# Linear attention: the product with the key-value state folded into the output weight, inverse denominators broadcast through DRAM; Mixer 1 held in program order

## The chip, the cores and the metric

The kernel runs on one core of one Trainium2 chip. The metric is the device time of one execution in microseconds (us). A kernel is timed in several rounds beside the kernel before on the same chip.

Engine names as the profile prints them: PE is TensorE (matmuls), PEld its weight loads, DVE is VectorE, ACT is ScalarE, POOL is GpSimd, SP is SyncE, which here only issues DMAs. L1163 is line 1163 of the kernel concerned; line numbers differ a little between the kernels.

## The reference, cut to what matters

A pre-normalised block: linear attention over 2048 tokens (width 1024, 32 heads of 32), then a token-mixing MLP with 3584 hidden features.

```python
phi = lambda t: jnp.where(t > 0, t + 1, jnp.exp(t)) + 1e-6
pq, pk = phi(q), phi(k)
kv  = jnp.einsum("bhsd,bhse->bhde", pk, v)          # one 32x32 state per head
z   = jnp.einsum("bhsd->bhd", pk)
num = jnp.einsum("bhqd,bhde->bhqe", pq, kv)
den = jnp.einsum("bhqd,bhd->bhq", pq, z)[..., None] + 1e-6
o   = num / den
h   = x + o.reshape(B, S, D) @ wo                   # q, k, v are projections of layernorm(x)
# Mixer: y = w2(gelu(w1(layernorm(h), over tokens) + b1)) + b2;   result = h + y
```

Because the division is by one number for each token and head, it may be done on `pq`, before both products. Then `kv` and `wo` can be multiplied together once, and the output projection takes the scaled `pq` directly.

## The kernel before

The work runs in this order on TensorE: keys and values with their state; the query projection in 32 units of eight matmuls (a unit is 512 tokens by 128 features); the attention product and the output projection in 16 row blocks of 128 tokens; Mixer 1 (2048 tokens to 3584 features, a seven-product matrix scheme nested in quads, five quads after the first pair); Mixer 2.

The attention product works on one row block: eight matmuls of 132 columns (numerator and denominator side by side), two small ScalarE operations for 1/den as exp(-ln), three VectorE products, and a transposing DMA back into `pqT`.

```python
def attn_num_den(i):
    for j in range(ND):                                   # 8 matmuls, 132 columns each
        nc.tensor.matmul(nd_ps[:, b, sl * NCOL:(sl + 1) * NCOL],
                         lhsT=pqT[:, j, i * P:(i + 1) * P], rhs=ndrhs[:, j, :], start=True, stop=True)
    nc.scalar.activation(dn..., nd_ps..., ACT.Ln, bias=eps_den[:], scale=1.0)
    nc.scalar.activation(rd[:], dn[:], ACT.Exp, scale=-1.0)
    ...                                                   # 3 VectorE products into o_sb
def attn_transpose(i, o_sb):
    nc.sync.dma_start_transpose(out=pqT[:, :, i * P:(i + 1) * P], in_=o_sb[:])

def out_proj(i):
    ...
    for dc in range(NDC):                                 # two halves of 512 columns
        ap_ = acc_tile()                                  # one of five PSUM tiles, in a ring
        nc.scalar.copy(ap_[:, 0:CW], xr[:, dc * CW:(dc + 1) * CW])     # seed: x into PSUM
        for j in range(ND):
            nc.tensor.matmul(ap_[:, 0:CW], lhsT=pqT[:, j, i * P:(i + 1) * P],
                             rhs=wo_sb[:, j, dc * CW:(dc + 1) * CW], ...)
        nc.scalar.copy(h_bf[:, dc * CW:(dc + 1) * CW], ap_[:, 0:CW])
        nc.vector.bn_stats(st[:, dc, :], ap_[:, 0:CW])
    nc.vector.bn_aggr(mv_all[:, i, :], st[:])
    nc.scalar.activation(lnv[:], mv_all[:, i, 1:2], ACT.Ln, ...)       # then Exp
    nc.sync.dma_start(h_dram[i][:], h_bf[:])

for (u, j) in q_units[8:]:
    q_unit(u, j)                                          # 8 matmuls, then phi on ScalarE and VectorE
    if u >= 1 and j % 2 == 1:
        i = (u - 1) * TPC + j // 2
        attn(i)
        ...                                               # loads of wo, then of w1
for i in range(NS):
    if i % 2 == 0 and i // 2 < TPC:
        attn(NS - TPC + i // 2)
    load_xr(i + XRL)                                      # cut: only while there are rows left
    out_proj(i)
    if i >= 2: normalize_h(i - 2)                         # layer norm, then combinations of row pairs
    ...
```

A scheduler sets each engine's order from this program. `pin(...)` holds an instruction in program order against the other pinned ones of its engine; what is not pinned may move.

## Time and profile before

572.96 us median of 3 runs (572.88 to 573.27). The profiled execution has a span of 571.5 us.

From the page: busy time by engine, then the busy share of TensorE and its granted clock in 40 equal slices, in tenths.

```profile
PE 563.7 (99%) x3124; PEld 293.3 (51%) x3124; DVE 390.2 (68%) x759; ACT 272.0 (48%) x585; POOL 1.8 (0%) x8
PE   7999999999999999999999999999999999999997
PEclk9999999999999999999999999999999999999999
```

TensorE is the limit: nothing pays that doesn't take time off it. The next view is the table of windows. I cut the span at four events in TensorE's trace: the last key-value matmul, the first matmul of Mixer 1, the first quad, the end of the quads and the first matmul of Mixer 2. Columns: window, length, then busy time (and instructions) of each engine, granted clock, DMA share, GB/s.

```profile
125.86:235.50 109.64, 109.64 (x604) 53.47 (x602) 85.99 (x208) 74.87 (x178) 0.00 (x0) 1.00 0.61 158
235.50:259.32 23.82, 22.93 (x106) 10.18 (x106) 18.33 (x35) 10.35 (x18) 0.00 (x0) 1.00 0.03 12
259.32:376.01 116.69, 116.52 (x673) 65.60 (x672) 62.90 (x129) 56.00 (x119) 0.00 (x0) 1.00 0.29 91
376.01:403.03 27.02, 27.02 (x153) 14.86 (x152) 10.37 (x19) 13.00 (x27) 0.00 (x0) 1.00 0.27 69
```

The first window is the attention stage (queries, attention product, output projection): 109.64 us, and TensorE is busy in all of it. The second is the start of Mixer 1, with 0.9 us of waiting. The third holds five quads, 22.42 us and then four of 23.57 us. "The stage", "the mixer start" and "the quads" mean these windows below.

TensorE's timeline around two attention groups (start, length, instruction, count):

```profile
150.23 0.63 PE L1118 MATMUL nd_ps<-ndrhs,pqT 128*128 128x132 bf16 x8
150.70 3.61 PE L1019 MATMUL acc_t<-xnT,wq_sb 128*128 128x512 bf16 x16
154.15 0.63 PE L1118 MATMUL nd_ps<-ndrhs,pqT 128*128 128x132 bf16 x8
```

A group of eight attention matmuls takes 0.47 us of TensorE's time (150.23 to 150.70); there are 16 groups, 7.5 us.

### The profile page before, as it was taken

To read this page: it belongs to the slowest core of one execution; us is meant where nothing else is said; L and a number is where in the kernel's file an instruction comes from. 1 tells how busy PE (TensorE), PEld (TensorE's weight loads), DVE (VectorE), ACT (ScalarE), POOL (GpSimd) and SP (SyncE) were. 2 spreads that over 40 slices of the span, in tenths; PEclk is the share of its full clock that TensorE was granted. 3 is DMA by queue.
4 is the path that set the end of the run, shared out by engine and by line. 5 is a ranking of instruction groups with operands and counts; after the bars stand their busy time and mean duration, and the time that the engine had idled before them with its cause. 6 is when DMAs were issued, how large, how long until landed. Compare 5 with 4: busy or idle time off the path is not lost.

```text
span 571.5 us, 8308 instructions
## 1 busy us (share of the span) xinstructions
PE 563.7 (99%) x3124; PEld 293.3 (51%) x3124; DVE 390.2 (68%) x759; ACT 272.0 (48%) x585; POOL 1.8 (0%) x8
## 2 busy tenths in 40 slices
PE   7999999999999999999999999999999999999997
PEld 3444444455554444346555565555445655645643
DVE  6898887546767879873735627453979749659625
ACT  4747777666667776445445354453220411311211
POOL 1000000000000000000000000000000000000000
PEclk9999999999999999999999999999999999999999
DMA  9933432029536753104041340413892932912111
GB/s 303 357 76 79 89 74 38 19 96 323 118 72 127 177 178 111 55 2 147 1 148 28 120 148 1 148 48 81 205 255 84 244 96 75 278 56 73 38 47 46
DMA packets 97800, 66.61 MB, mean 117 GB/s; under 512 B 32082, under 2 KB 91744, under 8 KB 97760
## 3 DMA queue, kind: packets, MB, share of 16 engines
q1 hardware_dynamic: 97024, 65.42, 41.7%
q10 hardware_dynamic: 672, 0.66, 0.3%
q8 instruction: 24, 0.39, 0.3%
q14 instruction: 16, 0.13, 0.1%
q0 software_dynamic: 64, 0.01, 0.0%
HBM read 50.34 MB, written 8.39 MB: 103 GB/s over the span
## 4 chain that ended last, share of the span: by engine, by line
PE 95%; DVE 3%; ACT 1%; issue 1%; DMA 1%; ACTq 0%
PE psB L297 10%; PE psC L297 10%; PE acc_t L1019 9%; PE acc_t L1167 9%; PE psC L208 7%; PE psA L297 7%; PE psI L230 7%; PE psB L208 6%; PE psI L208 6%; PE psB L750 4%; PE psC L750 4%; PE psA L750 4%; PE psA L208 3%; PE acc_t L674 2%; PE psE L750 2%; PE psE L297 1%
## 5 line engine op out<-in xcount | busy, mean ns | idle before, releaser
L297 PEld LDWEIGHTS <-sa 128*128 128x128 f16 x436 | 42.6, 98 | 46.8 <-issue 0.7
L1019 PE MATMUL acc_t<-xnT,wq_sb 128*128 128x512 bf16 x256 | 58.0, 379 | 0.0
L1167 PE MATMUL acc_t<-wo_sb,pqT 128*128 128x512 bf16 x256 | 56.1, 379 | 0.0
L208 PEld LDWEIGHTS <-wq 128*128 128x128 bf16 (+1 forms) x357 | 34.5, 98 | 31.3
L297 PEld LDWEIGHTS <-wq 128*128 128x128 bf16 (+1 forms) x324 | 31.6, 98 | 33.1 <-issue 1.0
L208 PE MATMUL psC<-gs,wq 128*128 128x512 f16 (+2 forms) x210 | 45.0, 365 | 0.0
L1167 PEld LDWEIGHTS <-pqT 128*128 128x128 bf16 x256 | 24.8, 98 | 29.0
L1019 PEld LDWEIGHTS <-wq_sb 128*128 128x128 bf16 x256 | 24.5, 98 | 27.4
L166 ACT ACTIVATE e_sb<-acc_t 128x512 bf16<-128x512 f32 x40 | 23.9, 597 | 26.5 <-PE acc_t L1019 24.3
L170 DVE TENSOR_SCALAR e_sb<-e_sb 128x512 bf16<-128x512 bf16 x64 | 18.5, 289 | 25.4 <-ACT e_sb L166 24.8
L208 PEld LDWEIGHTS <-sa 128*128 128x128 f16 x231 | 22.6, 98 | 18.6
L750 PEld LDWEIGHTS <-xs 128*128 128x128 f16 x208 | 20.0, 98 | 23.3 <-DVE xs L736 1.3
L208 DVE TENSOR_TENSOR ot<-ot,hr 128x512 bf16<-128x512 bf16 (+2 forms) x27 | 11.2, 415 | 28.1 <-ACT ot L406 27.7
L333 ACT COPY psC<-psB 128x512 f32<-128x512 f32 x22 | 12.5, 570 | 35.1 <-PE psB L297 21.5
L297 PE MATMUL psB<-hT,sa 128*128 128x512 f16 x112 | 28.4, 379 | 0.0
L441 DVE TENSOR_TENSOR e<-psI,es 128x256 f32<-128x256 f32 x12 | 5.1, 425 | 34.0 <-PE psI L230 34.0
L297 PE MATMUL psC<-hT,wq 128*128 128x512 f16 x112 | 28.3, 379 | 0.0
L750 PE MATMUL psA<-wkv,xnT 128*128 128x512 bf16 x104 | 26.7, 379 | 0.0
L1178 DVE BATCH_NORM_STATS2 hst<-acc_t 128x6 f32<-128x512 f32 x32 | 22.1, 692 | 6.7 <-ACT h_bf L1177 6.5
L297 PE MATMUL psA<-hO,wq 128*128 128x512 f16 x112 | 25.6, 379 | 0.7 <-ACT psB L316 0.7
L297 PE MATMUL psB<-hO,sa 128*128 128x512 f16 x112 | 25.5, 379 | 0.0
L297 PE MATMUL psC<-hT,sa 128*128 128x512 f16 x112 | 25.5, 379 | 0.0
(184 smaller groups left out, 1022.9 us busy)
## 6 DMA issues: line engine op xcount, KB each, us to landing
wq<-in_B_w_dram SPq DMA_DIRECT2D x14, 1024.0 KB, 7.7
wq<-in_B_w_dram SPq DMA_DIRECT2D x8, 1792.0 KB, 9.1
xr<-in_A_x_dram SPq DMA_DIRECT2D x16, 256.0 KB, 3.1
h_dram<-h_bf SPq DMA_DIRECT2D x16, 256.0 KB, 2.2
hr<-h_dram SPq DMA_DIRECT2D x32, 128.0 KB, 2.4
out_dram<-ot SPq DMA_DIRECT2D x31, 128.0 KB, 1.8
x_sb<-in_A_x_dram SPq DMA_DIRECT2D x15, 256.0 KB, 3.2
wkv<-in_A_wqkv_dram SPq DMA_DIRECT2D x2, 1024.0 KB, 9.0
```

Source lines behind the costliest of these rows:

```text
L166: pin(nc.scalar.activation(e_sb[:], src, ACT.Exp))
L170: pin(nc.vector.tensor_scalar(e_sb[:], e_sb[:], 1.0, PHI_EPS, ALU.min, ALU.add))
L208: return (lambda *a, **kw: pin(op(*a, **kw))) if Held.on else op
L230: pe.matmul(ps, lhsT=self.lhs[m][:, k, :], rhs=self.mov[m][:, k, :], start=(start and k == 0), stop=(k == self.nk - 1), skip_group_check=True,
L297: pe.matmul(ps[:, cols], lhsT=lhs[:, k, :], rhs=mv(k)[:, cols], start=(start and k == 0), stop=(k == self.nk - 1), skip_group_check=True,)
L333: nc.scalar.copy(self.C[:], self.B[:])
L441: dve.tensor_tensor(self.sts[m].e[:, self.cols(h)], ps, es, ALU.add)
L674: mm = nc.tensor.matmul(pp[:, 0:CW], lhsT=xnT[:, kt, i * P:(i + 1) * P], rhs=wkv[:, kt, c * CW:(c + 1) * CW], start=(kt == 0), stop=(kt == ...
L750: pin(nc.tensor.matmul(ps[:], lhsT=lhs[:, k, :], rhs=rhs[:, k, :], start=(start and k == 0), stop=(k == hk2 - 1), skip_group_check=True,))
L1019: nc.tensor.matmul(qp[:, 0:SW], lhsT=wq_sb[:, kt, j * P:(j + 1) * P], rhs=xnT[:, kt, u * SW:(u + 1) * SW], start=(kt == 0), stop=(kt == ND ...
L1167: nc.tensor.matmul(ap_[:, 0:CW], lhsT=pqT[:, j, i * P:(i + 1) * P], rhs=wo_sb[:, j, dc * CW:(dc + 1) * CW], start=(j == 0 and not SEED_RES ...
L1178: nc.vector.bn_stats(st[:, dc, :], ap_[:, 0:CW])
```

## The change

The intent is to take the 128 attention matmuls (and 48 VectorE products) away. The state is transposed and multiplied into the output weight once (`kv_transpose`, `fold`). The denominators of a chunk of 512 tokens come from eight matmuls of 32 output rows that can run four at a time in column groups of the array. Their inverses go to DRAM and come back broadcast over the 32 features of each head (`rdb`), and two VectorE products for each chunk scale `pqT` in place. Independently of this, the additions of Mixer 1's quads are held in program order. The diff, cut to its core:

```diff
-            def attn_num_den(i): ...          # 8 matmuls, Ln, Exp, 3 products
-            def attn_transpose(i, o_sb): ...
+            def kv_transpose():               # 8 transposes, one ScalarE copy
+                ...
+            def fold(j):
+                for c in range(NDC):
+                    ps = acc_tile()
+                    nc.tensor.matmul(ps[:, 0:CW], lhsT=kvT[:, j, :], rhs=wo_sb[:, j, cols], start=True, stop=True)
+                    ...                       # copied into wf by ScalarE (c == 0) or VectorE
+            def den(u):
+                ps = ndp.tile([P, SW], F32, tag="den", name="den_ps")
+                for o in range(2):
+                    for g in range(4):
+                        j = 4 * o + g
+                        nc.tensor.matmul(
+                            ps[g * QR:(g + 1) * QR, :],
+                            lhsT=zz[:, j, (1 - o) * HB:(1 - o) * HB + QR],
+                            rhs=pqT[:, j, u * SW:(u + 1) * SW], ...
+                            tile_position=(0, g * QR),
+                        )
+                nc.scalar.activation(ps[:], ps[:], ACT.Ln, bias=eps_den[:], scale=1.0 / S)
+                nc.scalar.activation(rd[:], ps[:], ACT.Exp, scale=-1.0)
+                pin(nc.sync.dma_start(rd_dram[u][:], rd[:]))
+                for h in range(2):
+                    rdb = a3d.tile([P, NH, SW], FP16, tag="rdb", bufs=3, name="rdb")
+                    for q in range(HB):
+                        pin(nc.sync.dma_start(rdb[q * DH:(q + 1) * DH, :, :], ... to_broadcast([DH, 4, SW])))
+                    rdbs[u, h] = rdb
+                    if 0 < u < 3:
+                        load_w1(u - 1, h, pin)            # 1 MB each
+            def scale_q(u, h):
+                v = pqT[:, h * NH:(h + 1) * NH, u * SW:(u + 1) * SW]
+                pin(nc.vector.tensor_tensor(v, v, rdbs.pop((u, h))[:], ALU.mult))
...
+            scale_at = {6: (0, 0), 7: (0, 1), 13: (1, 0), 14: (1, 1), 21: (2, 0), 22: (2, 1)}
+            for n, (u, j) in enumerate(q_units[8:]):
                 q_unit(u, j)
-                if u >= 1 and j % 2 == 1: attn(i) ...
+                if j == 0:
+                    den(u - 1)
+                if n == 1:
+                    kv_transpose()
+                if 4 <= n < 4 + ND:
+                    fold(n - 4)
+                if n in scale_at:
+                    scale_q(*scale_at[n])
             for i in range(NS):
-                if i % 2 == 0 and i // 2 < TPC: attn(NS - TPC + i // 2)
+                if i == 0:
+                    den(NSC - 1)
+                elif i in (3, 4):
+                    scale_q(NSC - 1, i - 3)
...
# Mixer 1: additions of a quad through `dve`, which is pinned while Held.on
-            nc.vector.tensor_tensor(t[:], ps[:], self.e[:], ALU.add)
+            dve.tensor_tensor(t[:], ps[:], self.e[:], ALU.add)
...
+    nxt.hold = pin
+    Held.on = True
     for u in range(1, NQ1):
         ...
+    Held.on = False
```

More of the change, by code (lines that the diff above doesn't have):

```diff
@@ L56 @@
     HB = P // DH
-    NCOL = P + HB
-    JPB = BANK // NCOL
-    NNB = (ND + JPB - 1) // JPB
+    QR = P // 4
+    assert ND == 8 and 3 * HB <= QR
     KPB = BANK // (P + 1)
@@ L100 @@
     for q in range(HB):
-        nc.vector.memset(maskbd[q * DH:(q + 1) * DH, q * DH:(q + 1) * DH], 1.0)
+        nc.vector.memset(maskbd[q * DH:(q + 1) * DH, q * DH:(q + 1) * DH], 1.0 / S)
         nc.vector.memset(m4[q * DH:(q + 1) * DH, q:q + 1], 1.0)
@@ L107 @@
     eps_den = const.tile([P, 1], F32)
-    nc.vector.memset(eps_den[:], DEN_EPS)
+    nc.vector.memset(eps_den[:], DEN_EPS / S)
     b1_rows = const.tile([NF, P], BF16)
@@ L134, in w_tile, with load_w1 @@
         return pool.tile([P, n], BF16, tag="wq", name="wq")
-    def load_w1(u, half):
+    def load_w1(u, half, hold=lambda ins: ins):
         if half == 0:
@@ L139, in load_w1 @@
         k = slice(half * NSP, (half + 1) * NSP)
-        nc.sync.dma_start(
+        hold(nc.sync.dma_start(
             w1_tiles[u][:, k, :],
             B_w1[:, u * CW:(u + 1) * CW].rearrange("(k p) f -> p k f", p=P)[:, k, :],
-        )
+        ))
     def load_w2(p, pool):
@@ L218, in __init__, with sums @@
             self.lhs = {1: self.a11, 2: self.a12, 4: self.a22}
-        def sums(self):
+        def sums(self, hold=lambda ins: ins):
             sm = [pools["is"].tile([P, self.nk, P], FP16, tag=self.tag, bufs=pools["is_bufs"], name="is")[:] for _ in range(4)]
-            dve.tensor_tensor(sm[0], self.a21, self.a22, ALU.add)
+            hold(dve.tensor_tensor(sm[0], self.a21, self.a22, ALU.add))
             dve.tensor_tensor(sm[1], sm[0], self.a11, ALU.subtract)
@@ L373, in evac_shared, with finish @@
             t = pools["t"].tile([P, BANK], F32, tag=f"t{fh}", name="t1")
-            nc.vector.tensor_tensor(t[:], ps[:], self.e[:], ALU.add)
+            dve.tensor_tensor(t[:], ps[:], self.e[:], ALU.add)
             self.evac(fh, 1, t)
+        todo = []
         def done(self):
-            e = gE[:, self.p, :]
-            nc.vector.tensor_tensor(e[:, CW:D], e[:, CW:D], e[:, 0:CW], ALU.subtract)
+            self.todo.append(gE[:, self.p, :])
+            if not Held.on:
+                self.finish()
+        def finish(self):
+            while self.todo:
+                e = self.todo.pop(0)
+                dve.tensor_tensor(e[:, CW:D], e[:, CW:D], e[:, 0:CW], ALU.subtract)
     class Mixer2(Product7):
@@ L422, in __init__ @@
             self.mov1, self.mov5 = mov1, mov5
+            self.hold = lambda ins: ins
         def cols(self, h):
@@ L445, in pre @@
                 self.in1 = Inner(self.sts, 1, self.mov1, "i1", self.sink1, self.sum1)
-                self.in1.sums()
+                self.in1.sums(self.hold)
             for st in self.sts:
@@ L530, in run @@
             interleave(self.in5, [st.p6 for st in self.sts])
+            self.sts[0].finish()
             pre = nxt.pre if nxt is not None else (lambda m: None)
@@ L585 @@
         a3s = actx.enter_context(tc.tile_pool(name="a3s", bufs=4))
-        a3w = actx.enter_context(tc.tile_pool(name="a3w", bufs=3))
-        a3o = actx.enter_context(tc.tile_pool(name="a3o", bufs=3))
+        a3d = actx.enter_context(tc.tile_pool(name="a3d", bufs=1))
         hstat = actx.enter_context(tc.tile_pool(name="hstat", bufs=1))
@@ L594 @@
         pqT = pqpool.tile([P, ND, S], BF16)
-        ndrhs = pqpool.tile([P, ND, NCOL], BF16)
+        kvbd = pqpool.tile([P, ND, P], BF16)
+        zz = pqpool.tile([P, ND, QR + HB], BF16)
         xctx = ExitStack()
@@ L1084 @@
                 q_fill()
+            nc.vector.memset(zz[:, :, 0:3 * HB], 0.0)
+            nc.vector.memset(zz[:, :, 3 * HB:], float(S))
             for b in range(NKB):
@@ L1087 @@
                 nc.vector.tensor_tensor(
-                    ndrhs[:, j0:j0 + n, 0:P],
+                    kvbd[:, j0:j0 + n, :],
                     kv_ps[b][:, 0:n, 0:P],
@@ L1093 @@
                 nc.vector.tensor_tensor(
-                    ndrhs[:, j0:j0 + n, P:NCOL],
+                    zz[:, j0:j0 + n, HB:2 * HB],
                     kv_ps[b][:, 0:n, P:P + 1].to_broadcast([P, n, HB]),
@@ L1101 @@
         warmctx.close()
+        kvT = xctx.enter_context(tc.tile_pool(name="kvtpool", bufs=1)).tile([P, ND, P], FP16, name="kvT")
         wpool = sactx.enter_context(tc.tile_pool(name="wpool", bufs=2, side="right"))
@@ L1109 @@
         ndp = a3p.enter_context(tc.tile_pool(name="ndp", bufs=1, space=PSUM))
-        nd_ps = ndp.tile([P, NNB, BANK], F32, name="nd_ps")
-        nc.vector.memset(nd_ps[:], 0.0)
+        rd_dram = [dram.tile([P, SW], FP16, name=f"rd_dram{u}") for u in range(NSC)]
         with ExitStack() as a3:
-            def attn_num_den(i):
+            def kv_transpose():
+                tp = ndp.tile([P, ND, P], BF16, tag="tp", name="kvtp")
                 for j in range(ND):
-                    b, sl = divmod(j, JPB)
-                    nc.tensor.matmul(
-                        nd_ps[:, b, sl * NCOL:(sl + 1) * NCOL],
-                        lhsT=pqT[:, j, i * P:(i + 1) * P],
-                        rhs=ndrhs[:, j, :],
-                        start=True,
-                        stop=True,
-                    )
-                dn = a3s.tile([P, NNB * JPB * HB], F32, name="dn")
-                nc.scalar.activation(
-                    dn[:].rearrange("p (b s c) -> p b s c", b=NNB, c=HB),
-                    nd_ps[:, :, 0:JPB * NCOL].rearrange("p b (s c) -> p b s c", c=NCOL)[:, :, :, P:NCOL],
-                    ACT.Ln,
-                    bias=eps_den[:],
-                    scale=1.0,
-                )
-                rd = a3s.tile([P, NNB * JPB * HB], F32, name="rd")
-                nc.scalar.activation(rd[:], dn[:], ACT.Exp, scale=-1.0)
-                o_sb = a3o.tile([P, D], BF16, name="o_sb")
-                for b in range(NNB):
-                    nsl = min(JPB, ND - b * JPB)
-                    blk = nd_ps[:, b, 0:nsl * NCOL].rearrange("p (s c) -> p s c", c=NCOL)
-                    nc.vector.tensor_tensor(
-                        o_sb[:, b * JPB * P:(b * JPB + nsl) * P].rearrange("p (s h e) -> p s h e", h=HB, e=DH),
-                        blk[:, :, 0:P].rearrange("p s (h e) -> p s h e", e=DH),
-                        rd[:, b * JPB * HB:(b * JPB + nsl) * HB].rearrange("p (s h) -> p s h", h=HB).unsqueeze(3).to_broadcast([P, nsl, HB, DH]),
-                        ALU.mult,
-                    )
-                return o_sb
-            def attn_transpose(i, o_sb):
-                nc.sync.dma_start_transpose(out=pqT[:, :, i * P:(i + 1) * P], in_=o_sb[:])
@@ new lines, in kv_transpose @@
+                    nc.tensor.transpose(tp[:, j, :], kvbd[:, j, :], ident[:])
+                nc.scalar.copy(kvT[:], tp[:])
+            wf = wo_sb[:].bitcast(FP16)
+            def fold(j):
+                for c in range(NDC):
+                    cols = slice(c * CW, (c + 1) * CW)
+                    ps = acc_tile()
+                    nc.tensor.matmul(ps[:, 0:CW], lhsT=kvT[:, j, :], rhs=wo_sb[:, j, cols], start=True, stop=True)
+                    if c == 0:
+                        nc.scalar.copy(wf[:, j, cols], ps[:, 0:CW])
+                    else:
+                        nc.vector.tensor_copy(wf[:, j, cols], ps[:, 0:CW])
@@ new lines @@
+            rds = {}
+            rdbs = {}
+            NH = ND // 2
+            def den(u):
[6 more added lines that the diff above has]
+                            lhsT=zz[:, j, (1 - o) * HB:(1 - o) * HB + QR],
+                            rhs=pqT[:, j, u * SW:(u + 1) * SW],
+                            start=(o == 0),
+                            stop=(o == 1),
+                            skip_group_check=True,
+                            tile_position=(0, g * QR),
+                        )
+                rd = a3d.tile([P, SW], FP16, tag="rd", name="rd")
+                nc.scalar.activation(ps[:], ps[:], ACT.Ln, bias=eps_den[:], scale=1.0 / S)
[3 more added lines that the diff above has]
+                    rdb = a3d.tile([P, NH, SW], FP16, tag="rdb", bufs=3, name="rdb")
+                    rows = rd_dram[u].rearrange("(g o h) n -> o h g n", g=4, h=HB)
+                    for q in range(HB):
+                        pin(nc.sync.dma_start(
+                            rdb[q * DH:(q + 1) * DH, :, :],
+                            rows[h, q].unsqueeze(0).to_broadcast([DH, 4, SW]),
+                        ))
+                    rdbs[u, h] = rdb
+                    if 0 < u < 3:
+                        load_w1(u - 1, h, pin)
@@ L1169, in out_proj @@
                             lhsT=pqT[:, j, i * P:(i + 1) * P],
-                            rhs=wo_sb[:, j, dc * CW:(dc + 1) * CW],
+                            rhs=wf[:, j, dc * CW:(dc + 1) * CW],
                             start=(j == 0 and not SEED_RESIDUAL),
@@ L1192, in normalize_h @@
                     combine(hE[:, q, :], hO[:, q, :], hT2[:, q, :], hT3[:, q, :], hT4[:, q, :])
-            def attn(i):
-                attn_transpose(i, attn_num_den(i))
             TPC = SW // P
+            for c in range(NDC):
+                load_wo(c)
             for i in range(XRL):
                 load_xr(i)
-            for (u, j) in q_units[8:]:
+            scale_at = {6: (0, 0), 7: (0, 1), 13: (1, 0), 14: (1, 1), 21: (2, 0), 22: (2, 1)}
+            for n, (u, j) in enumerate(q_units[8:]):
                 q_unit(u, j)
-                if u >= 1 and j % 2 == 1:
-                    i = (u - 1) * TPC + j // 2
-                    attn(i)
-                    if i % 2 == 1 and i // 2 < 2:
-                        load_wo(i // 2)
-                    elif i % 2 == 1 and i // 2 < 6:
-                        load_w1(*divmod(i // 2 - 2, 2))
+                if j == 0:
[6 more added lines that the diff above has]
+                    scale_q(*scale_at[n])
             xctx.close()
+            a3w = a3.enter_context(tc.tile_pool(name="a3w", bufs=3))
             hpool = mctx.enter_context(tc.tile_pool(name="hpool", bufs=1, side="right"))
@@ L1217 @@
             for i in range(NS):
-                if i % 2 == 0 and i // 2 < TPC:
-                    attn(NS - TPC + i // 2)
+                if i == 0:
+                    den(NSC - 1)
+                elif i in (3, 4):
+                    scale_q(NSC - 1, i - 3)
                 if i + XRL < NS:
```

## The prediction

> **What bounds the kernel now.** TensorE. The page gives PE 563.7 of 571.5 us busy (99%), DVE 68%, ACT 48%, and puts 95% of the chain of waits on PE at a granted clock near 1. By the timeline, 512-column matmuls start 0.216 us apart, 256-column ones 0.108 and the 132-column attention ones 0.058. Against those spacings PE loses 9 us: 5 in the first 40 us, 1.5 at the start of mixer 1 (236 to 241 us: two waits, for DVE hE and for the ACT copy psB), 0.8 in the first quad (261 to 270), and 0.2 in each of five later quads.
>
> **Removed on PE.** 128 attention matmuls (numerator with denominator, 132 columns): the chain shows two query units every 3.92 us with a group of eight in between, 3.45 without it, so 0.47 us a group, 16 groups, 7.5 us, all on the critical path. Off it: 48 DVE products (25 us), 32 small ACT operations, 16 DMA transposes.
>
> **Added on PE.** 8 transposes of 128 columns (about 0.055 each, 0.45 us); 16 fold matmuls of 512 columns (3.45 us); 32 denominator matmuls of 512 columns, in four column groups of the array. One after another those would be 6.9 us. The Trainium skill ("TensorEngine Tiling (Array Packing)", Key Properties) says that tiles run in parallel and that a change of tiling mode drains the array, which no trace here shows yet. With four at a time and a drain of about 0.15 us at each end (estimate: 0.38 us duration less 0.216 spacing), eight cost about 0.9 us. The built order keeps the first two groups whole but splits the third as 7+1 and the fourth as 1+5+1+1, so I add some drains: about 4.8 us. Sum of this stage: -7.5 + 8.7 = about +1.2 us (between -1 and +4).
>
> **Waits.** The inverse denominators go through DRAM: write (2.2 us by the landing times of h), then a broadcast of 1 MB per 512 tokens in 1 KB rows (1 MB of w1 lands in 7.7 us). The second and third chunks share the queue with w1, so their second halves should land some us after the product wants them; DVE will idle up to 5 us there. Five PSUM tiles and four phi buffers cover it: under 0.5 us of PE wait.
>
> **Mixer 1.** The built PE order puts seven psE matmuls ahead of psA, so the waits at its start mostly close (-1.1); the first quad, reordered too, gains about 0.4; program order in the quads recovers perhaps half of 1.0. Total -2.0 us.
>
> **Predicted: 571.4 us**, range 568.0 to 575.0; faster by over 2%: 0.01, within 2%: 0.96, slower by over 2%: 0.03.
>
> **Right or wrong if:** denominator matmuls start well under 0.216 us apart within a group, a group occupying 0.7 to 1.1 us; fold matmuls 0.216 us apart; the stretch from the end of the key-value accumulation to the start of mixer 1 (126 to 235.5 us) grows by -1 to +4; PE's wait for psB at mixer 1's start shrinks from 0.7 us; DVE idle before the products, released by a DMA; quads of 23.4 us instead of 23.57.
>
> **What would make it wrong:** the column groups running one by one (+3 us or more); a DVE stall on the broadcast that reaches PE through the next denominator; a late output weight ahead of the first fold; conversely drains near zero (2 us less).

## The result, and the profile after

The changed kernel takes 593.06 us median (591.89 to 595.2, 4 runs), against 573.08 us (572.88 to 573.27) of the kernel before in the same rounds. The ratio is 1.0353, 95% interval 1.0323 to 1.0383: slower by 3.5%. A ratio here is the mean time of one kernel's fast runs over that of the other's fast runs of the same rounds, so it is not quite the ratio of the medians quoted.

The same lines of the page, of the kernel after (span 591.1 us):

```profile
PE 568.2 (96%) x3036; PEld 289.3 (49%) x3052; DVE 384.5 (65%) x728; ACT 273.2 (46%) x570; POOL 1.8 (0%) x8
PE   8999999999998869989999999999999999999997
PEclk9999999999998989999999999999999999999999
```

TensorE, which was the limit, now has slices of 8 and 6, and its clock has slices of 8. The windows after, cut at the same events:

```profile
125.84:249.29 123.45, 113.72 (x526) 49.48 (x530) 77.44 (x170) 77.27 (x163) 0.00 (x0) 0.97 0.50 143
249.29:274.34 25.05, 22.61 (x105) 10.17 (x104) 20.08 (x40) 10.26 (x18) 0.00 (x0) 1.00 0.05 18
274.34:395.06 120.72, 117.26 (x673) 65.61 (x672) 62.34 (x127) 54.60 (x118) 0.00 (x0) 1.00 0.28 88
395.06:422.55 27.49, 27.25 (x153) 14.83 (x152) 11.65 (x21) 13.26 (x27) 0.00 (x0) 1.00 0.27 68
```

Window by window against before: the stage +13.81, the mixer start +1.23, the quads +4.03, the rest of Mixer 1 +0.47 us: 19.54 of the 19.6 us by which the profiled spans differ. Mixer 2 takes the same time. So time is lost in three places, and most of it in the stage.

**In the stage**, TensorE was busy for all of 109.64 us before. Now it is idle for 9.73 us (123.45 less 113.72) and busy for 4.08 us more. TensorE's waits from the stage to the mixer start (what waited, for what; us in total, times, longest):

```profile
PE acc_t L1199 <- ACT acc_t L1197: 4.5, 2, 2.8
PE acc_t L1199 <- DVE hE L155: 4.4, 1, 4.4
PE psE L296 <- DVE hE L155: 2.4, 1, 2.4
PE den_ps L1153 <- DVE pqT L170: 0.4, 1, 0.4
```

The first two are output-projection matmuls, in which the new work no longer takes part. Where they happened, on TensorE's timeline (in brackets the idle time before, and what ended it):

```profile
182.19 7.24 PE L1199 MATMUL acc_t<-wo_sb,pqT 128*128 128x512 f16 x25 [1.61 <-ACT acc_t L1197]
201.57 10.52 PE L1199 MATMUL acc_t<-wo_sb,pqT 128*128 128x512 f16 x48 [2.84 <-ACT acc_t L1197]
216.53 7.67 PE L1199 MATMUL acc_t<-wo_sb,pqT 128*128 128x512 f16 x27 [4.44 <-DVE hE L155]
```

The matmuls after the first and third gap run slower, too. Two windows of 3.40 us, right after the first gap and a little later (columns as in the other windows):

```profile
182.20:185.60 3.40, 3.40 (x9) 0.56 1.09 296
186.40:189.80 3.40, 3.40 (x17) 1.00 1.11 253
```

Nine matmuls against seventeen, at a granted clock of 0.56. Eight starts in a row are 0.427 us apart instead of 0.216, here and again at 216.7: 2 x 8 x 0.211 = 3.4 us. That is most of the 4.08 us of additional busy time, so the work itself grew by only about 0.7 us.

What came before the first gap is on ScalarE's timeline. Three lines, of the Ln of the third chunk's denominator, the first of the phi operations that had piled up, and the seeds of the output projection:

```profile
173.50 0.66 ACT L1163 ACTIVATE den_ps<-den_ps,eps_den 128x512 f32<-128x512 f32 x1 [6.57 <-PE den_ps L1153]
...
174.69 0.59 ACT L165 ACTIVATE e_sb<-acc_t 128x512 bf16<-128x512 f32 x1
...
181.37 2.80 ACT L1197 CAST acc_t<-xr 128x512 f32<-128x512 bf16 x5
```

The built order gives TensorE seven of the third chunk's eight denominator matmuls, then 31 query matmuls, then the eighth. ScalarE's Ln needs the eighth. It stands in ScalarE's queue ahead of the phi operations of the query units that TensorE computes meanwhile, so ScalarE sits idle for 6.57 us with work behind it. It then works through seven units of phi, and the first seeds come at 181.37, when TensorE has nothing else left. The Trainium skill, "Perfetto Trace Analysis" (section "Tensor Engine Instruction (MATMUL, LD_WEIGHTS)"), calls the queues of ACT and DVE strict FIFO. The 6.57 us agree with that.

The second gap has the same cause: the last matmul of the fourth chunk's split group comes alone at 198.36, ScalarE's Ln waits 1.79 us for it, and the seeds stand behind that Ln. The third and longest gap is different. The profile puts it down to `hE`, which these matmuls don't read; the seed that they do need ended at 216.48, just before they started. It stood in ScalarE's queue behind the Ln of a row block, which waited 2.62 us for VectorE's statistics, and VectorE had run one of the new products (212.40, 1.22 us) ahead of these. Two lines of ScalarE's timeline:

```profile
198.77 0.66 ACT L1163 ACTIVATE den_ps<-den_ps,eps_den 128x512 f32<-128x512 f32 x1 [1.79 <-PE den_ps L1153]
...
214.50 0.29 ACT L1213 ACTIVATE hln_l<-mv_all,eps 128x1 f32<-128x1 f32 x1 [2.62 <-DVE mv_all L1211]
```

VectorE has a stall of its own a little earlier, for the second half of the second chunk's broadcast:

```profile
167.19 1.23 DVE L1180 TENSOR_TENSOR pqT<-pqT,rdb 128x2048 bf16<-128x2048 bf16 x1 [3.11 <-DMA rdb<-rd_dram]
```

The first four broadcast DMAs of this chunk land 2.9 to 3.5 us after issue; the last four, issued after 1 MB of w1, land 8.1 to 8.7 us after issue.

**At the mixer start** TensorE's timeline shows the new order. Before (two lines) and after (two lines):

```profile
237.34 0.38 PE L297 MATMUL psA<-hE,wq 128*128 128x512 f16 x1 [0.15 <-DVE hE L1189]
239.96 1.02 PE L297 MATMUL psA<-hO,wq 128*128 128x512 f16 x4 [0.74 <-ACT psB L316]
```

```profile
255.35 0.38 PE L296 MATMUL psE<-hE,sa 128*128 128x512 f16 x1 [2.44 <-DVE hE L155]
256.00 1.03 PE L296 MATMUL psA<-hO,wq 128*128 128x512 f16 x4
```

The eighth psE matmul needs the last row pair. Before, it came after the four psA matmuls on hO; now it comes ahead of them, and they cannot fill the wait.

**In the quads** TensorE is idle for 3.46 us (120.72 less 117.26) against 0.17. The first quad takes 22.80 us (before: 22.42), the four later ones 23.57, 25.16, 24.86 and 24.34 us (before: 23.57 each). One reason stands on VectorE's timeline: the first addition on newly loaded w1 in the second quad, which prepares the third, before and after:

```profile
296.49 0.43 DVE L222 TENSOR_TENSOR is<-wq 128x512 f16<-128x512 bf16 x1 [2.22 <-DMA wq<-in_B_w_dram]
```

```profile
313.19 0.42 DVE L207 TENSOR_TENSOR is<-wq 128x512 f16<-128x512 bf16 x1 [2.85 <-DMA wq<-in_B_w_dram]
```

In the four quads from the second on, the second half of w1 lands 9.17, 8.87, 8.36 and 8.12 us after issue, the first three times ahead of a slow quad, the last ahead of the rest of Mixer 1; before it was 7.7 to 7.9 in all but the last load (8.04). The DMA view of one such load, before (312 to 320 us) and after (329 to 338 us), with queue, packets, MB and share of the DMA engines:

```profile
q1 hardware_dynamic: 2080, 2.10, 82.9%
```

```profile
q1 hardware_dynamic: 2080, 2.10, 71.7%
q8 instruction: 1, 0.02, 0.8%
```

After the change, a fetch of TensorE's instructions (16 KB) falls into the middle or the start of each of these loads. Before, it fell outside or into a load's last microsecond. The experiments below test whether that is the cause.

### The profile page after: what moved, and what is told of

The parts are those of the page before. It is cut to its first block, busy times and chain, and to the rows that moved or that the text cites. A ratio compares the mean times of both kernels' runs of the same rounds, so it can differ in the third digit from the quotient of the medians.

```text
span 591.1 us, 8106 instructions
## 1 busy us (share of the span) xinstructions
PE 568.2 (96%) x3036; PEld 289.3 (49%) x3052; DVE 384.5 (65%) x728; ACT 273.2 (46%) x570; POOL 1.8 (0%) x8
## 4 chain that ended last, share of the span: by engine, by line
PE 72%; DVE 13%; ACT 6%; DMA 6%; issue 2%; SPq 0%; DVEq 0%
PE psC L207 10%; PE psB L207 10%; PE psI L207 9%; PE acc_t L1028 8%; PE psA L207 5%; DMA wq<-in_B_w_dram 4%; PE psB L759 4%; PE psC L759 4%; PE psA L759 4%; PE psB L296 3%; PE psA L296 3%; PE psC L296 2%; DVE hst L1210 2%; PE acc_t L683 2%; PE acc_t L1199 2%
## 5 line engine op out<-in xcount | busy, mean ns | idle before, releaser
L207 PEld LDWEIGHTS <-wq 128*128 128x128 bf16 (+1 forms) x613 | 59.5, 98 | 50.4 <-issue 0.4
L207 PEld LDWEIGHTS <-sa 128*128 128x128 f16 x591 | 57.8, 98 | 49.7
L1199 PE MATMUL acc_t<-wo_sb,pqT 128*128 128x512 f16 x256 | 59.3, 395 | 8.9 <-ACT acc_t L1197 4.5
L207 PEld LDWEIGHTS <-is 128*128 128x128 f16 x360 | 35.1, 97 | 21.5 <-issue 7.9
L1028 PEld LDWEIGHTS <-wq_sb 128*128 128x128 bf16 x256 | 24.7, 98 | 30.1 <-issue 1.3
L207 DVE TENSOR_TENSOR ot<-ot,hr 128x512 bf16<-128x512 bf16 (+2 forms) x27 | 11.2, 415 | 28.1 <-ACT ot L413 27.7
L207 PE MATMUL psB<-hT,sa 128*128 128x512 f16 x96 | 24.6, 379 | 0.0
L759 PEld LDWEIGHTS <-xnT 128*128 128x128 bf16 x156 | 15.3, 98 | 18.5 <-issue 0.2
L166 ACT ACTIVATE r_sb<-acc_t 128x512 bf16<-128x512 f32 x40 | 24.3, 607 | 0.0
L1197 ACT CAST acc_t<-xr 128x512 f32<-128x512 bf16 x32 | 18.4, 615 | 11.7 <-DVE hst L1210 9.7
L239 ACT COPY psI<-psI 128x256 f32<-128x256 f32 x18 | 6.5, 362 | 37.4 <-PE psI L207 37.4
L366 ACT ACTIVATE gO<-t,b_sb 128x512 f16<-128x512 f32 x14 | 10.1, 722 | 28.7 <-DVE t L207 26.0
```

Of the source, the lines that this page charges most:

```text
L166: pin(nc.scalar.activation(r_sb[:], src, ACT.Relu))
L207: return (lambda *a, **kw: pin(op(*a, **kw))) if Held.on else op
L759: pin(nc.tensor.matmul(ps[:], lhsT=lhs[:, k, :], rhs=rhs[:, k, :], start=(start and k == 0), stop=(k == hk2 - 1), skip_group_check=True,))
L1028: nc.tensor.matmul(qp[:, 0:SW], lhsT=wq_sb[:, kt, j * P:(j + 1) * P], rhs=xnT[:, kt, u * SW:(u + 1) * SW], start=(kt == 0), stop=(kt == ND ...
```

## The experiments

Twelve kernels were run. All twelve gave correct results.

### 1. Each half of the change alone

`e1_attention_alone` is the changed kernel with Mixer 1 as it was; `e2_hold_alone` is the kernel before with the held quads.

```diff
 # e1: from the kernel after                # e2: from the kernel before
-    nxt.hold = pin                         +    nxt.hold = pin
-    Held.on = True                         +    Held.on = True
     for u in range(1, NQ1): ...                 for u in range(1, NQ1): ...
-    Held.on = False                        +    Held.on = False
```

> The attention part with the mixer 1 quads back in the scheduler's order, as in the kernel before. If the two parts lose time each on its own (my theory): about 588.6 us, the stretch from the last key-value matmul to mixer 1 still near 123.5 us (109.6 in the kernel before), quads back at 23.57 us. Rival: the quads lost time only because the attention part hands them a late or disturbed start (a later w1, a shifted DMA): then this is as slow as the whole change, about 593 us, with quads of 24 to 25 us.

Measured: 591.79 us (589.43 to 593.51), ratio 1.0321 [1.0293, 1.0348].

> The kernel before with only the mixer 1 hold. My theory: the hold by itself puts the next quad's sums ahead of the additions that release PSUM on VectorE, so quads of 24.3 to 25.2 us and about 577.5 us in all. Rival (the attention part disturbs the quads): 573 us and quads of 23.57 or shorter. If the hold does what the change intends: 571 to 572 us.

Measured: 574.71 us (574.60 to 575.16), ratio 1.0028 [1.0011, 1.0045].

My expectation, that the halves share the loss with some microseconds for the hold, was a miss. The attention part alone brings nearly all of it, and its quads are slow as well (24.53, 24.73 and 23.87 us) though it doesn't touch them. The hold alone costs about 1.6 us. In e2, two additions that write the same single-buffered tile come one behind the other. The second waits for ScalarE to have read the first; this is VectorE's timeline:

```profile
282.84 0.69 DVE L208 TENSOR_TENSOR t<-psB,e 128x512 f32<-128x512 f32 x1 [0.79 <-ACT gE L367]
```

### 2. Denominators whole, and w1 away from the broadcasts

`e3_den_whole` holds the denominator groups, the query units and the first two output blocks in program order, and places each group one unit later, so that its phi is ready. `e4_w1_apart` takes the w1 loads out from between the two halves of a broadcast and issues them after a product.

```diff
 # e3
-                        nc.tensor.matmul(
+                        pin(nc.tensor.matmul(              # in den, in q_unit, in out_proj for i < 2
-                if j == 0:
+                if j == 1:
                     den(u - 1)
-                if i == 0:
+                if i == 1:
                     den(NSC - 1)
 # e4
-                    if 0 < u < 3:
-                        load_w1(u - 1, h, pin)
+                    if n in (14, 22):                      # in the loop of query units, after scale_q
+                        load_w1({14: 0, 22: 1}[n], 0, pin)
+                        load_w1({14: 0, 22: 1}[n], 1, pin)
```

> The whole change, but the denominator matmuls of a chunk come one query unit later (the last ones one output tile later) and are held together in program order on TensorE. Theory A: the harm is the denominator group that the scheduler split; ScalarE, whose logarithm stands in order behind it, idles 6.6 us, then is late with the copies that seed the output projection. Then the stretch from key-value to mixer 1 falls from 123.5 to 110 to 113 us and the whole to about 581. Theory B: the harm is the round trip of the inverses through DRAM, which stalls VectorE whatever TensorE's order is: then 589 to 593 us and VectorE still waits for rdb.

Measured: 586.83 us (586.34 to 589.70), ratio 1.0247 [1.0222, 1.0272]; the stage 117.49 us.

> The whole change, with the w1 loads moved from between the two halves of the broadcast to after its products. Theory B (the broadcast is late because w1 shares its queue): VectorE's wait for rdb (3.1 us) vanishes and the time falls by 8 us or more, to 585 or less. Theory A: VectorE's wait vanishes too, but in the built order the eighth denominator matmul still stands 17 matmuls behind its group and the last group is split, so ScalarE still idles about 3.5 us before the logarithm and the time falls by only 2 to 4 us, to 589 to 591.

Measured: 590.82 us (588.74 to 592.39), ratio 1.0304 [1.0278, 1.0331]; the stage 123.06 us.

Repairing the order takes 6.0 us off the stage, though it is not repaired everywhere: the fourth group still comes as seven and one, 24 matmuls apart, and ScalarE waits 3.4 us for the eighth. The run doesn't tell what the other pins (query units, output blocks) do by themselves. Now the late broadcast shows: VectorE waits 5.7 us for it, and TensorE 3.7 us, through the phi that the next denominator needs. Two lines of e3's waits, VectorE's and TensorE's:

```profile
DVE pqT L1180 <- DMA rdb<-rd_dram: 5.7, 1, 5.7
PE den_ps L1153 <- DVE pqT L170: 3.7, 1, 3.7
```

In e4 VectorE has no wait for a broadcast at all, and yet only 0.4 us of the stage goes in its trace (which is of its slowest run, 1.6 us above its median), because the split denominators still delay ScalarE. TensorE's waits of e4, and the ScalarE copy in the first of them:

```profile
PE acc_t L1197 <- ACT acc_t L1195: 8.0, 2, 4.3
196.81 1.07 ACT L1207 CAST h_bf<-acc_t 128x512 bf16<-128x512 f32 x2 [2.67 <-DMA h_dram<-h_bf]
```

Here the delay also runs through SyncE's queue: the copy waits for a store of h, which SyncE issued at 194.61, right behind the write of the fourth chunk's inverses at 194.17. That write waited for the Ln, and the last lone denominator matmul before it came at 192.44.

`e5_den_and_w1` does both:

> Both repairs of the attention part at once (denominators whole and one unit later; w1 out of the broadcast), the mixer hold left in. Each alone left the other cause standing: with den whole TensorE still waited 3.7 us for a phi behind the late broadcast, with w1 apart 8.0 us for ScalarE behind the split group. If these two are the causes: no wait above 1 us for rdb or in the denominator, no stretch at half clock, the stretch from key-value to mixer 1 111 to 113 us (117.5 with den whole alone) and 580 to 582 us in all. If a third cause is at work: 585 us or more.

Measured: 585.15 us (582.71 to 587.94), ratio 1.0202 [1.0172, 1.0233]; the stage 112.23 us, which is 11.2 us less than after the change. The two single effects on the stage add up to 6.4. That does not show that each cause hid behind the other: the same attention code has a stage of 123.45, 121.56 and 119.87 us in the traces of the kernel after, e1 and e7, so one trace can be off by some microseconds. In medians of the whole kernel, each against the kernel before of its own rounds, the savings are 6.4 us (e3), 2.4 (e4) and 8.3 (e5): about the sum. In e5, too, the fourth group is seven and one, and ScalarE waits 2.7 us for the eighth. What is left of e5's 12 us lies in the mixer start (27.80 us), the quads, and 3 us of waits in the output projection:

```profile
PE psE L296 <- DVE hE L155: 3.1, 1, 3.1
PE acc_t L1197 <- ACT acc_t L1195: 3.0, 2, 1.8
```

### 3. Instruction fetches inside the w1 loads

In the built program the change takes 144 of TensorE's instructions (weight loads and matmuls) away, ahead of the quads. The trace of the kernel before has 24 fetches and 6248 matmuls and weight loads, about one for 260. If a fetch comes after every so many instructions, that moves each fetch against the w1 loads. This can be tried without the change: `e6_before_56_fillers` adds 56 matmuls of 8 columns (112 instructions) to the warm-up of the kernel before, and `e7_attention_72_fillers` adds 72 (144 instructions) to e1.

```diff
+        for t in range(56):                                # 72 in e7
+            pin(nc.tensor.matmul(tiles[t % 5][:, 0:8], lhsT=warm[:, 0:P], rhs=warm[:, 0:8], start=True, stop=True))
```

> The kernel before with 56 tiny matmuls (112 TensorE instructions) after the warm-up and nothing else. Theory C: the mixer 1 quads of the attention kernels are slow because a 16 KB fetch of TensorE's instructions (one every 256 instructions, about 1.1 us on one DMA engine) now falls inside each w1 load, whose last packets land 1.3 us later; the change took 144 instructions away, and 112 more put the fetches at the same places modulo 256. Then w1 lands 9.0 to 9.4 us after its issue (7.7 to 7.9 before), mixer 1 takes 170.5 to 172 us (167.5 before), all after a start 1 to 3 us later. Theory D: the quads are slow for something the attention code leaves behind (memory places, queue state): mixer 1 stays at 167.5 us.

Measured: 575.43 us (575.09 to 576.19), ratio 1.0035 [1.0019, 1.0052]. Three of the quads grow from 23.57 to 24.16, 24.24 and 24.08 us, and the second half of w1 lands 8.7 to 9.0 us after issue. The start of the kernel costs only 0.12 us more. In the load at 312 us there is now a fetch (DMA view, 312 to 321 us):

```profile
q8 instruction: 1, 0.02, 0.8%
```

> The attention part alone (no hold) with 72 tiny matmuls (144 TensorE instructions) after the warm-up, which brings TensorE's instruction count at mixer 1 back to that of the kernel before. Theory C: w1 lands 7.7 to 8.0 us after issue again and the quads take 23.57 us (24.5, 24.7, 23.9 without the fillers); mixer 1 about 171 us, of which its late start is the rest. Theory D: quads stay at 24 to 25 us.

Measured: 590.43 us (589.53 to 591.12), ratio 1.0292 [1.0276, 1.0308]. The quads are at 23.57 us, all four, with w1 in 7.8 to 7.9 us where e1 had 9.2, 9.4 and 8.5. The stage starts 2.4 us later in this profiled run (TensorE is at half clock from 8.8 to 12.2 us), so the total gains little. The two runs move the quads both ways, with the quads' own code untouched: the place of the fetch is the cause.

`e8_hold_alternate` goes with these. It keeps the hold, but interleaves other additions between the two that share a tile:

```diff
-            for st in self.sts:
-                st.p7(...)
+            for st, n in zip(self.sts, new):
+                st.p7(...)
+                if n is not None:
+                    n.asum(7)                              # the same for p3 and asum(3)
```

> The hold alone, with the four last sums of the next quad put between the additions (addition, sum, addition, sum) instead of after each pair, in program order. Theory E: the hold loses 1.6 us because two additions in a row share one single-buffered tile, so the second waits 0.79 us for ScalarE's GELU of the first, and GELU is then late in front of the copies that the inner products wait for. Then quads of 23.57 us again, mixer 1 at 167.5 us and about 573.2 us in all. Otherwise it stays near 574.7 us.

Measured: 573.62 us (573.46 to 574.00, 5 runs), ratio 1.0001 [0.9988, 1.0013], quads of 22.80 and four times 23.57. So the shared tile was the hold's cost, and without it the hold gains nothing either.

### 4. All repairs together

`e9_all_repairs` starts from e5: no hold of the quads, the first mixer pair's TensorE order pinned as written, six output blocks pinned, later products (by two query units for the first two chunks, in the output blocks for the last two), and 56 fillers. With six output blocks pinned, all four groups are whole. In `e10_last_chunk_own_queue`, GpSimd's queue issues the last chunk's write and broadcast, so that SyncE's queue is not blocked for the loads of x behind them.

```diff
 # e9
-    Held.on = True ... Held.on = False
+    Held.first = True                                      # pins TensorE's instructions only
     pend = run_pair(cur, [], nxt)
+    Held.first = False
+                if i in (1, 2): scale_q(NSC - 2, i - 1)
+                if i in (7, 8): scale_q(NSC - 1, i - 7)
 # e10, on top
-                pin(nc.sync.dma_start(rd_dram[u][:], rd[:]))
+                eng = nc.gpsimd if u == NSC - 1 else nc.sync
+                pin(eng.dma_start(rd_dram[u][:], rd[:]))   # and the eight broadcasts
```

> The folded attention with every named cause taken away at once: denominators in whole groups held in program order, w1 loads away from the broadcasts, later products for the last two chunks, the first mixer pair's TensorE order held as written, no hold of the quads, and 56 small filler matmuls so that the instruction fetches fall outside the w1 loads. Theory (the named causes are all of the loss): last key-value matmul to first mixer matmul 109 to 111 us, from there to the quads at most 24.5 us, quads of 23.57, and 572 to 575 us (before plus 0 to 2). Rival (a third cause, for instance the broadcasts' traffic itself or SyncE's queue blocked behind the last reciprocal's write): the stage still 112 us or more, 577 us or more.

Measured: 576.92 us (576.73 to 578.71, 5 runs), ratio 1.0064 [1.0049, 1.0079].

> As the run of all repairs, with the last chunk's reciprocal write and broadcast issued from GpSimd's queue, so that the loads of x and the stores of h behind them in SyncE's in-order queue are not blocked. Theory (the named causes are all): within 0.5 us of the run of all repairs. Rival (SyncE's blocked queue is a remaining cause): 0.5 to 2 us less, and the TensorE waits in the output projection, 1.4 and 2.0 us in the run of whole groups and separate loads, gone.

Measured: 575.01 us (574.87 to 575.46, 5 runs), ratio 1.0021 [1.0008, 1.0035]: 1.3 us slower than the kernel before, where the changed kernel was 20 us slower. The windows of e10:

```profile
126.09:238.34 112.25, 110.28 (x532) 48.81 (x530) 78.68 (x175) 77.77 (x163) 5.00 (x9) 0.98 0.51 159
238.34:260.79 22.45, 22.45 (x106) 10.17 (x104) 18.18 (x36) 10.15 (x18) 0.00 (x0) 1.00 0.03 12
260.79:377.47 116.68, 116.51 (x674) 65.63 (x672) 62.70 (x129) 55.74 (x119) 0.00 (x0) 1.00 0.29 91
```

The quads are as before and the mixer start is 1.4 us shorter than before (22.45 against 23.82, no wait left). It is 22.45 in e12 as well, but 24.12 in e9 and 24.51 in e11, whose TensorE order there is the same. The stage is still 2.6 us longer. In it there is one wait, and 7 matmul starts at half clock after it (7 x 0.211 = 1.5 us); TensorE's waits of e10:

```profile
PE acc_t L1200 <- ACT acc_t L1198: 2.0, 1, 2.0
```

Counted from start to start (less the usual 0.216 us) the gap is 2.1 us; with the slow starts that is 3.6 us. Without them the stage would be about 108.6 us, 1.0 us less than before (an estimate from these numbers).

The theory that the named causes were all has failed by these 2.6 us of the stage. The rival of e10, a blocked queue, forecast 0.5 to 2 us less than e9, and the medians are 1.9 us apart. But the stage is 112.2 us in both traces: e9 has two waits of 2.0 and 1.5 us in it at full clock, e10 one of 2.0 us with the slow starts. The traces differ at the mixer start (24.12 against 22.45 us) and before the stage, where e9's profiled run was unlucky: it was 1.4 us above its own median, its warm-up at half clock until 10 us. So what the queue costs in e9 stays open.

### 5. Two attempts at the last wait

In e10 the seed that TensorE waits for stands in ScalarE's queue behind the Ln of an earlier block, which waits for VectorE's statistics. In `e11_products_after_statistics`, the chunk products come after these statistics. In `e12_seeds_a_block_ahead`, the seeds are pinned one block ahead.

```diff
 # e11, against e10
-                if i in (1, 2): scale_q(NSC - 2, i - 1)
-                if i in (7, 8): scale_q(NSC - 1, i - 7)
+                if i in (4, 5): scale_q(NSC - 2, i - 4)
+                if i in (8, 10): scale_q(NSC - 1, i // 2 - 4)
 # e12, against e10
+                if i == 0: seed(0)
+                if i + 1 < NS: seed(i + 1)                 # seed(): the two pinned copies of x into PSUM
-                    nc.scalar.copy(ap_[:, 0:CW], xr[:, dc * CW:(dc + 1) * CW])
```

> As the run with the last chunk on its own queue, but the third chunk's two products come after the statistics of the third row block on VectorE, not in front of them, and the fourth chunk's a block or two later. That run kept one TensorE wait of 2.0 us at 192.9 us, for a ScalarE seed held up behind VectorE's statistics, followed by seven matmuls at half rate (1.5 us). Theory (the product in front of the statistics makes that wait): the wait falls below 0.7 us, no matmuls at half rate follow, the stage comes to 108.6 to 110 us and the kernel to 571.5 to 573.5 us, at or a little under before. Rival (the combinations of the first row pair or the late row loads of x make it): the wait stays at 1.5 us or more, the stage at 111.5 us or more.

Measured: 577.37 us (577.18 to 577.40), ratio 1.0070 [1.0056, 1.0083]; the stage 111.92 us. No matmuls at half clock, but three gaps in the output projection, of 1.5, 1.3 and 0.6 us from start to start.

> As the run with the last chunk on its own queue, with each row block's two ScalarE seeds of PSUM emitted and held one block ahead of its matmuls, so that no seed stands behind the row statistics of the block before in ScalarE's in-order queue. Moving the products behind the statistics did not remove the wait (three waits of 1.5, 1.3 and 0.6 us came in place of one of 2.1). Theory (seeds queued behind the statistics make the last TensorE waits): all waits in the output projection together below 0.7 us, the stage 108.6 to 109.6 us, the kernel 571 to 573 us, 0 to 2 us under before. Rival (ScalarE, VectorE or the row loads are too slow for the output projection at this point, whatever the order): waits of 1.5 us or more remain, the stage at 111 us or more.

Measured: 577.78 us (577.46 to 579.12, 6 runs), ratio 1.0082 [1.0070, 1.0095]; the stage 114.48 us. TensorE's waits of e12:

```profile
PE acc_t L1209 <- ACT acc_t L1196: 4.6, 5, 1.7
```

Both theories fell: a change of order moves the wait and does not remove it. Consistent with that, VectorE is busy for 14.6 to 16.9 of the 20 us from 190 to 210 in e10 to e12, with ScalarE and VectorE waiting for each other in turn. But before, it was busy for 16.5 of 20 there with no wait of TensorE at all, so load alone doesn't explain it. What would close this last wait stays open. None of the versions beats the kernel before.

## Why the prediction was wrong, point by point

The predicted time of 571.4 us, range 568 to 575, was wrong: 593.06 us.

- **The work on TensorE: right.** The prediction said "about +1.2 us (between -1 and +4)". The four whole denominator groups in e10 take 0.64 us each (0.309 from the last query matmul to the first of the group instead of 0.216, then 0.548 to the next ordinary one). With them the sum is -7.5 + 0.45 + 3.45 + 4 x 0.64 = -1.0 us, which is what e10's stage gives without its gap. In the built order of the kernel after, the splits add four lone matmuls at about 0.42 us each, hence about +0.7.
- **Four at a time: right.** Within a group the starts are 3 to 4 ns apart and the second four start 0.227 us after the first four. That agrees with the Trainium skill, "TensorE: Matmul & The Clock Gate" (section "Part 3: Packing small matmuls — row/col tiling"), which gives about 4 ns between tiles. Entering and leaving the mode costs 0.19 us for a group (0.64 less two passes of 0.227). I had put a whole group at 0.9.
- **"Five PSUM tiles and four phi buffers cover it: under 0.5 us of PE wait": this step failed.** TensorE idles for 9.7 us in the stage. I had seen the splits 7+1 and 1+5+1+1 in the built order, and costed them as drains on TensorE. Their cost is on ScalarE: an in-order queue whose head waits for the eighth matmul, 6.57 us in the third chunk and 1.79 in the fourth. Holding the order takes 6.0 us off the stage (e3). The longest single gap, 4.4 us, comes from seeds behind the row statistics on VectorE; it is of the kind that e10 to e12 did not remove.
- **"DVE will idle up to 5 us there": right in size, wrong in reach.** VectorE did idle, 3.1 us in the kernel after and 5.7 in e3. But this reaches TensorE (3.7 us in e3), which I had only listed among what would make the prediction wrong. Both causes together are worth 11.2 us of the stage in the trace and 8.3 us of the kernel by the medians (e5).
- **Not in the prediction at all: the clock.** TensorE ran 16 matmuls at half rate after gaps, 3.4 us.
- **"The built PE order puts seven psE matmuls ahead of psA, so the waits at its start mostly close (-1.1)": this step failed.** I counted the seven and not the eighth, which needs the last row pair: +1.2 us, a wait of 2.4. The order costs only where VectorE is late with that pair: in e4, with the same order of TensorE there, the wait is 0.6 us and the mixer start 23.19 us. With the order as written pinned, the start shortens by 1.4 us in e10 and e12, but not in e9 and e11.
- **"The first quad gains about 0.4; program order in the quads recovers perhaps half of 1.0": this step failed.** The first quad took 22.80 us instead of 22.42. The hold costs 1.6 us alone (e2), by two writes in a row to one tile, and gains nothing once that is mended (e8). The rest of the slower quads (e6, e7) comes from the place of the instruction fetches, of which I knew nothing.

## What to carry to other kernels

Before costing a new operation by the engine that runs it, ask which in-order queue will hold its consumer, and what stands behind that consumer: here one matmul that came 31 matmuls late held up ScalarE for 6.57 us, and with it everything behind. When two suspected causes lie in the same stage, try them together as well as alone, and compare medians of the whole kernel beside the stage of one trace: here the stage of the same code varied by 3.6 us from trace to trace. And where a change adds or removes instructions, compare the untouched stages too: their fetches have moved.

## What the Trainium skill lacked or had wrong

- "Runtime: NRT & Kernel Launch" (section "Instruction fetch mechanics") gives 16 KiB blocks of 256 instructions, fetched by the sequencer's own DMA queue, and calls the cost mostly hidden. The trace agrees on the size (one fetch of 0.02 MB every 22 us or so in the quads, about one for 260 recorded instructions). What it lacks is that a fetch holds up a bulk load that it falls into: the second MB of a load of w1 landed 8.4 to 9.4 us after issue (kernel after, e1, e6) instead of 7.7 to 7.9, and a quad took 23.9 to 24.7 us (e1, e6) instead of 23.57. One such fetch took about 1.1 us.
- "TensorE: Matmul & The Clock Gate" (section "HAM oscillation — how this bites in real kernels") gives the rule of no idle gaps over about 3.4 us. Here half clock followed gaps of 1.6 us (kernel after) and 2.0 us (e10), while a gap of 2.8 us (kernel after) and gaps of 2.0 and 1.5 us (e9) were not followed by it; what decides it stays open. The length of the slow stretch, about 3.4 us (eight starts of 0.427 us), agrees with the window of about 3.4 us that the page gives for both directions (section "What's actually happening").
- "TensorEngine Tiling (Array Packing)" (section "Key Properties") says that a change of mode drains the array, and gives no figure. Here a group of eight in four column groups cost 0.19 us more than its two passes.
- No page that I found gives the time of a small broadcast that is queued behind a bulk load: a 128 KB broadcast from DRAM landed 2.9 to 4.0 us after issue with no load ahead of it (kernel after, first chunk and first half of the second), and 8.1 to 8.7 us after issue behind 1 MB of w1 on the same queue (second half of the second chunk; 5.8 to 9.4 us over the kernel after, e1, e3 and e7).
